# Copies of packed heads from gl into pkt: issued on GpSimd in place of VectorE

## The chip, the cores and the metric

The program runs on one core of a Trainium2 chip, in one launch. The metric is the device time of one execution in microseconds (us). The engines are named as in the profile: PE is TensorE's matmul stream and PEld its weight loads, DVE is VectorE, ACT is ScalarE, POOL is GpSimd, SP is SyncE, which here only issues DMAs. POOL issues DMAs too.

## The reference

Three layers follow each other. The first packs the sequence into 32 rows for each head and attends to them:

```python
def sm_attn(qq, kk, vv):                      # softmax attention, scale 1/8
    ...
p_packed = sm_attn(p, k, v)                   # (4, 8, 32, 64): 32 packed rows per head
out = sm_attn(q, p_packed, p_packed)          # q: (4, 8, 576, 64)
```

The second is a mixture of 4 experts on the 2304 tokens (512 wide, 1024 hidden): `out += p[:, e] * (relu(x @ w1[e]) @ w2[e])`. The third is a soft mixture: `logits = x @ phi` (32 slots), a softmax over the tokens gives 32 slot inputs, each goes through one of 8 experts of the same shape, and a softmax over the slots distributes the results. All is float32, and the result is (2304, 512).

## The kernel before

The work is cut into 4 batches `b` of 576 tokens, and the 8 heads of a batch into two groups `g` of 4. Order is written out by hand: each engine runs its instructions in the order in which the Python code issues them, and waits on semaphores where a tile comes from another engine.

`attention(b, g, ...)` is a generator, one `yield` for each step. For one group its steps are, in the code's order: transpose p and both halves of k (DVE L305, L288), scores of the packed rows into the PSUM tile `sa` (PE L297), softmax, transposed probabilities into `etm` (ACT L336), packed heads into the PSUM tile `pv` (PE L346) and from there into `gl` (ACT L357). Then come the 8 copies of L366: four heads by two halves of the head's width, each 32 partitions by 32 columns, from partitions 64*(h%2)+32*dh of `gl` to partitions 32*h of `pkt`, which becomes a block matrix with zeros between. After them both halves of q are transposed (DVE L288), multiplied with `pkt` into the PSUM tile `sb` (PE L297), turned into `nat` (DVE L378), normalized by a second softmax (L385 to L395, POOL for the differences and products), transposed into `a2` (L400) and split into a high and a low part (L409, L410). `gl` has two buffers, one for even and one for odd batches; `pkt` has one part for each group.

The attention of batches 0's two groups runs first, in the order of the string HEAD, mixed with the preparation of `wphi`. From then on there is a main loop of 128 slots, 32 for each batch. One slot does `mm1` (12 matmuls of L473 into two PSUM tiles `h`, ACT's L477 into `ht`), and at every fourth slot `make_g` (16 matmuls of L443 into two PSUM tiles `g`, split by ACT L454 and DVE L455) and `logits` (L500). `flip_h` transposes the `ht` of an earlier slot into `hn` (DVE L483) and scales it there (POOL L484). In the same slots one step of each attention generator of the next batch runs: group 0 starts at slot 0 of 32, group 1 at slot 9 (OFF1). So the 8 copies come twice in a batch, six times in the loop. The PSUM tiles for `h`, `g`, `sa`, `sb` and `pv` take turns in four banks, so that a matmul into a bank waits until its last reader is done. The order inside a slot is that of the string ORDER:

```python
    ORDER = "FGLMSAP"    # flip, make_g, logits, mm1, softmax step, attention step, pool_slots
```

The loads of q, k, v and p for later groups are issued on POOL (L136, L143), from the list `due` that is worked off at the start of the next slot; a k, q or v tile is one of four buffers, so an issue waits for the last reader of its buffer. w1 comes through SP (L169). When a batch is done, `pool_slots` (PE L611) multiplies its `hn` into the slot sums. After the loop, the rest of the weights streams in through SP (L715) into buffers that the loop has freed, and the last layers are computed (L989 to L1124).

Of the kernel before, what the change touches and what calls it, by code (L numbers as in the profile page):

```python
# [18 lines left out]
def tile_packed_attention_moe_softmoe(  # L19
# [15 lines left out]
    pe, act, dve, pool, sp = nc.tensor, nc.scalar, nc.vector, nc.gpsimd, nc.sync  # L35
# [242 lines left out]
    def attention(b, g, feeds, ptb, pkb, etb, tmp, gp):  # L278
# [83 lines left out]
        for h in range(4):  # L362
            for dh in range(2):
                src = 64 * (h % 2) + 32 * dh
                o = 32 * (2 * ((h + g) % 2) + h // 2)
                dve.tensor_copy(  # L366
                    pkb[32 * h : 32 * h + 32, dh, o : o + 32],
                    glb[src : src + 32, 2 * g + h // 2, :],
                )
# [46 lines left out]
    def start_attention(b, g):  # L416
        feeds = {}
        nb, ng = (b, 1) if g == 0 else (b + 1, 0)

        def later(src, nm, hf, bb, gg):  # L420
            return lambda: load_half(src, nm, bb, gg, hf)

        for hf in range(2):
            feeds[f"q{hf}"] = later(q, "q", hf, b, g)
            if nb < NB:
                feeds[f"k{hf}"] = later(k, "k", hf, nb, ng)
                feeds[f"v{hf}"] = later(v, "v", hf, nb, ng)
        if nb < NB:
            f = feeds["k0"]
            feeds["k0"] = lambda: (load_p(nb, ng), f())  # L430
        return attention(b, g, feeds, pt, pkt[:, g], [etm], att_tmp, pool)
# [305 lines left out]
    with tc.manual_schedule():  # L737
# [58 lines left out]
        def head_tmp(tag, name):  # L796
            if tag == "kt":
                return ht_pool.tile([128, S], F32, tag="ht", name=name)
            return spare[tag]

        gens = {
            "0": attention(0, 0, {}, pt, pkt[:, 0], [etm, et_x[0]], att_tmp, dve),
            "1": attention(
                0, 1, {}, pp1, pkt[:, 1], [et1, et_x[1]], head_tmp,
                pool if GP1 == "pool" else dve,
# [347 lines left out]
```

## Time and profile before

| | |
|---|---|
| device time, 3 runs | median 549.1 us (548.97 to 549.73) |
| the profiled execution | 549.31 us, span 547.2 us, granted TensorE clock 0.983 of full speed |
| PE busy | 498.7 us, 91% of the span |
| DVE busy | 322.2 us, 59% |
| ACT busy | 240.0 us, 44% |
| POOL busy | 236.3 us, 43% |

The span runs from the first to the last instruction; the device time has some 2 us around it. A busy share is an average over stages with different limits: the head (to about 50 us), the loop (to about 440 us) and the tail, in which weights stream in. The chain of waits follows the instruction that ended last back to what released it, step by step. An idle time in brackets in a timeline is that of the engine just before the instruction, with what ended it.

### The profile page before, as it was taken

Reading aid. Unit: us, or ns where it says so; the run is one execution under the profiler, and the core shown is the slowest. Engines: PE = TensorE matmul, PEld = TensorE weight load, DVE = VectorE, ACT = ScalarE, POOL = GpSimd, SP = SyncE. Lnnn points to the kernel's source line nnn. Section 1 sums busy time; section 2 is a strip of 40 time slices with the busy share of each in tenths; the row PEclk is TensorE's granted clock in tenths of the full one; section 3 lists DMA queues with packets and bytes.
Section 4 is the critical chain, followed back from the end, with each engine's and each line's share of the span. In section 5 each row is a group of like instructions: output and inputs, shape, how many; then the busy total and the mean of one; then the engine's idle time right before and its main releaser. Section 6 shows DMA issues by size and latency. Waiting matters only on the chain.

```text
span 547.2 us, 12839 instructions
## 1 busy us (share of the span) xinstructions
PE 498.7 (91%) x5356; PEld 347.5 (63%) x5356; DVE 322.2 (59%) x623; ACT 240.0 (44%) x548; POOL 236.3 (43%) x246
## 2 busy tenths in 40 slices
PE   7898999989999999899998989999999977998882
PEld 5776787867865767687556768775787853222132
DVE  6475457776767776768776676666645434451051
ACT  3766564655452447365334654551454411120041
POOL 8212445676642557675335555842555612000000
PEclk9998999999999999999999999999999997998998
DMA  8997155352430443443205432360388369999998
GB/s 283 365 375 271 49 166 176 98 166 79 153 122 1 146 143 103 150 148 120 79 10 177 158 100 79 132 234 22 126 277 292 128 238 398 409 389 383 371 253 239
DMA packets 70874, 104.06 MB, mean 190 GB/s; under 512 B 4433, under 2 KB 50257, under 8 KB 70817
## 3 DMA queue, kind: packets, MB, share of 16 engines
q1 hardware_dynamic: 66992, 93.20, 49.2%
q0 software_dynamic: 3232, 9.75, 6.0%
q8 instruction: 42, 0.69, 0.5%
q10 hardware_dynamic: 592, 0.29, 0.2%
q14 instruction: 16, 0.12, 0.1%
HBM read 98.52 MB, written 4.72 MB: 189 GB/s over the span
## 4 chain that ended last, share of the span: by engine, by line
PE 54%; DVE 15%; DMA 14%; ACT 8%; issue 4%; POOL 3%; SPq 0%; POOLq 0%; DVEq 0%; ACTq 0%
PE h L473 26%; DMA ck<-in_moe_w_dram 7%; PE sl L611 6%; PE g L443 5%; PE lg L500 4%; DMA hn<-in_moe_w_dram 3%; DVE pkt L366 3%; PE sb L297 3%; ACT etm L336 3%; DMA k<-in_k_dram 3%; PE sa L297 2%; PE w2t L251 2%; DVE hn L483 2%; POOL hn L484 2%; PE pw L237 1%
## 5 line engine op out<-in xcount | busy, mean ns | idle before, releaser
L473 PE MATMUL h<-a,g 128*128 128x288 f32 x1536 | 227.6, 302 | 6.9 <-DVE g L455 4.5
L473 PEld LDWEIGHTS h<-a,g 128*128 128x128 f32 x1536 | 208.7, 188 | 33.4 <-issue 22.3
L484 POOL TENSOR_TENSOR hn<-hn,dp_sb 128x576 f32<-128x576 f32 x128 | 152.0, 1193 | 130.0 <-DVE hn L483 126.3
L477 ACT ACTIVATE ht<-h 128x288 f32<-128x288 f32 x256 | 103.7, 412 | 155.2 <-PE h L473 154.9
L483 DVE STREAM_TRANSPOSE hn<-ht 128x576 f32<-128x576 f32 x128 | 96.3, 758 | 50.2 <-ACT ht L477 50.0
L455 DVE TENSOR_TENSOR g<-g,g 128x512 fp32r<-128x512 f32 x64 | 41.1, 683 | 24.8 <-ACT g L454 24.8
L611 PE MATMUL sl<-hn,dpt 32*32 32x512 f32 x1152 | 48.2, 597 | 2.4 <-DVE dpt L572 2.0
L454 ACT CAST g<-g 128x512 fp32r<-128x512 f32 x64 | 34.3, 588 | 21.1 <-PE g L443 21.0
L500 PE MATMUL lg<-ht,wphi 128*32 128x288 f32 x512 | 37.8, 412 | 0.0
L443 PE MATMUL g<-w,gl 64*32 64x512 f32 x512 | 35.7, 601 | 0.4 <-ACT ht L477 0.2
L611 PEld LDWEIGHTS sl<-hn,dpt 32*32 32x32 f32 x1152 | 21.0, 103 | 22.3 <-issue 13.3
L500 PEld LDWEIGHTS lg<-ht,wphi 128*32 128x32 f32 x512 | 13.5, 109 | 32.7 <-issue 25.5
L366 DVE COPY pkt<-gl 32x32 f32<-32x32 f32 x64 | 22.8, 356 | 7.3 <-ACT gl L357 6.5
L346 PE MATMUL pv<-etm,v 128*64 128x64 f32 x468 | 19.0, 225 | 6.5 <-ACT etm L336 3.4
L410 POOL TENSOR_TENSOR a<-a,a 64x576 fp32r<-64x576 f32 x14 | 20.0, 1427 | 9.6 <-ACT a L409 8.8
L336 ACT COPY etm<-et 32x288 f32<-32x288 f32 x52 | 22.2, 428 | 1.6 <-DVE et L330 0.4
L346 PEld LDWEIGHTS pv<-etm,v 128*64 128x64 f32 x468 | 16.2, 137 | 10.6 <-ACT etm L336 5.7
L1074 PE MATMUL so<-hn,tacc 128*32 128x384 f32 (+1 forms) x80 | 18.5, 590 | 2.7 <-DMA hn<-in_moe_w_dram 2.5
L629 DVE TENSOR_TENSOR tacc<-sl,tacc 128x512 f32<-128x512 f32 (+2 forms) x32 | 15.3, 545 | 9.4 <-PE sl L611 9.4
L297 PE MATMUL sa<-k,pt 128*128 128x288 f32 x56 | 16.9, 428 | 3.7 <-DVE k L288 3.6
L256 ACT COPY hn<-w2t 128x512 f32<-128x512 f32 x32 | 17.3, 588 | 6.6 <-PE w2t L251 6.5
L251 PE MATMUL w2t<-ident,hn 128*128 128x128 f32 x128 | 18.3, 287 | 1.8 <-ACT hn L256 1.3
(180 smaller groups left out, 492.4 us busy)
## 6 DMA issues: line engine op xcount, KB each, us to landing
w<-in_moe_w_dram SPq DMA_DIRECT2D x32, 1024.0 KB, 5.4
hn<-in_moe_w_dram SPq DMA_DIRECT2D x42, 512.0 KB, 9.7
ck<-in_moe_w_dram SPq DMA_DIRECT2D x42, 512.0 KB, 8.0
hn<-in_moe_w_dram SPq DMA_DIRECT2D x14, 384.0 KB, 8.5
q<-in_q_dram POOLq DMA_DIRECT2D x12, 288.0 KB, 3.2
out_dram<-ob SPq DMA_DIRECT2D x11, 288.0 KB, 4.4
k<-in_k_dram POOLq DMA_DIRECT2D x10, 288.0 KB, 3.2
v<-in_v_dram POOLq DMA_DIRECT2D x10, 288.0 KB, 3.6
```

What stands on the lines that cost most here:

```text
L297: pe.matmul(ps[:, :HS], lhs[:, j, :], t[:, :, j, :], start=(j == 0), stop=(j == 1))
L336: act.copy(etb[hf % len(etb)][r, h % 2, :, 32 * (h // 2) : 32 * (h // 2) + 32], et[r, HB * hf : HB * hf + HB, :],)
L346: pe.matmul(pv[64 * par : 64 * par + 64, :64], vn[:, x, :], etb[hf % len(etb)][:, par, x, :], start=(hf == 0 and x == 0), stop=(hf == 1 an ...
L366: dve.tensor_copy(pkb[32 * h : 32 * h + 32, dh, o : o + 32], glb[src : src + 32, 2 * g + h // 2, :],)
L443: pe.matmul(pss[g][32 * ((c + 2 * g) % 4) : 32 * ((c + 2 * g) % 4) + 32, :], gl[b % 2][r, c, :], t[r, c], start=True, stop=True, tile_posi ...
L455: dve.tensor_tensor(out=lo, in0=pss[g], in1=hi.bitcast(F32), op=ALU.subtract)
L473: pe.matmul(ps[:, :HS], gg[:, l, g, e % 2, fs], r[:, ts], start=(g == 0 and t == 0), stop=(g == 1 and t == 2),)
L477: act.activation(out=ht[:, ts], in_=ps[:, :HS], func=AF.Relu)
L483: dve.transpose(out=own, in_=unturned.pop((n, kf, e)).rearrange("p (x t) -> p x t", t=32))
L484: pool.tensor_tensor(out=own, in0=own, in1=dp_sb[:, n // NU, :, e].unsqueeze(2).to_broadcast([128, NBLK, 32]), op=ALU.mult,)
L500: pe.matmul(lg_t[b, pr][32 * c : 32 * c + 32, :HS], wphi[:, 2 * i + kf, 32 * e : 32 * e + 32], ht_t[n, kf, e][:, HS * hf : HS * hf + HS], ...
L611: pe.matmul(pss[f][c : c + 32, :], dpt[r, x, :], hn[r, p0 : p0 + NU, x, 2 * ep : 2 * ep + 2].rearrange("p n e k f -> p n (e k f)"), start= ...
```

## The change

One line: the 8 copies of each group are issued on POOL's queue.

```diff
         for h in range(4):
             for dh in range(2):
                 src = 64 * (h % 2) + 32 * dh
                 o = 32 * (2 * ((h + g) % 2) + h // 2)
-                dve.tensor_copy(
+                pool.tensor_copy(
                     pkb[32 * h : 32 * h + 32, dh, o : o + 32],
                     glb[src : src + 32, 2 * g + h // 2, :],
                 )
```

The 64 copies leave DVE's order and enter POOL's at the same place of the code. The orders of ACT and SP stay as they are; PE's too, but its `sb` matmuls now wait for POOL's semaphore where they took `pkt` from DVE.

DVE's order in the loop, where group 1 of batch 1 copies (`ht_0_1`, `ht_1_0` and `ht_1_1` are outputs of `mm1`, `q_1523` is the first transposed half of q):

```order
 L483 STREAM_TRANSPOSE hn<-ht_0_1_1427 128x18x32 [waits Activation_49]
 L483 STREAM_TRANSPOSE hn<-ht_1_0_1452 128x18x32 [waits Activation_49]
-L366 COPY pkt<-gl_114 32x32 [waits Activation_49]
-L366 COPY pkt<-gl_114 32x32 x7
 L288 STREAM_TRANSPOSE q_1523<-q_1157 128x576 [waits DMASW5_49]
 L483 STREAM_TRANSPOSE hn<-ht_1_1_1498 128x18x32 [waits Activation_49]
```

The transposes of q and of `ht_1_1`, and the two L455 behind them, now follow the transpose of `ht_1_0` directly.

POOL's order at the same place of the program (`k_1494` and `v_1525` are loads for batch 2, L484 scales `hn`):

```order
 L143 DMA k_1494<-in_k_dram 128x576 [waits DMASW0_49,PE_49]
 L484 TENSOR_TENSOR hn<-hn,dp_sb 128x18x32 [waits DVE_49,Pool_49]
+L366 COPY pkt<-gl_114 32x32 [waits Activation_49]
+L366 COPY pkt<-gl_114 32x32 [waits Pool_49]
+L366 COPY pkt<-gl_114 32x32 x6
 L143 DMA v_1525<-in_v_dram 128x576 [waits DMASW5_49,DVE_49]
-L484 TENSOR_TENSOR hn<-hn,dp_sb 128x18x32 [waits DVE_49]
+L484 TENSOR_TENSOR hn<-hn,dp_sb 128x18x32 [waits DVE_49,Pool_49]
```

The copies stand behind a load of k and a scaling, and in front of a load of v and the next scaling.

DVE's order where group 0 of batch 1 copies (`k_1153` and `k_1188` are the transposed halves of k for group 1, `q_1186` is the first of q for group 0):

```order
 L288 STREAM_TRANSPOSE k_1153<-k_1060 128x576 [waits DMASW3_49]
 L483 STREAM_TRANSPOSE hn<-ht_0_1_1113 128x18x32 [waits Activation_49]
-L366 COPY pkt<-gl_114 32x32 [waits Activation_49]
-L366 COPY pkt<-gl_114 32x32 x7
 L288 STREAM_TRANSPOSE q_1186<-q_803 128x576 [waits DMASW0_49]
 L288 STREAM_TRANSPOSE k_1188<-k_1155 128x576 [waits DMASW4_49,DVE_49]
```

The second half of k, which group 1's `sa` matmuls read, now stands two transposes behind the first.

## Rows read from the trace of the kernel before

**Rows 1.** The profile's page, part 4: the chain's shares of the span, by line.

```profile
PE h L473 26%; DMA ck<-in_moe_w_dram 7%; PE sl L611 6%; PE g L443 5%; PE lg L500 4%; DMA hn<-in_moe_w_dram 3%; DVE pkt L366 3%; PE sb L297 3%; ACT etm L336 3%; DMA k<-in_k_dram 3%; PE sa L297 2%; PE w2t L251 2%; DVE hn L483 2%; POOL hn L484 2%; PE pw L237 1%
```

**Rows 2.** The page, part 5: group xcount | busy us, mean ns | idle before, releaser.

```profile
L484 POOL TENSOR_TENSOR hn<-hn,dp_sb 128x576 f32<-128x576 f32 x128 | 152.0, 1193 | 130.0 <-DVE hn L483 126.3
```

**Rows 3.** Line L366: engine op xcount: ns min/median/max, first and last start us.

```profile
L366 DVE COPY pkt<-gl x64: 126/174/1637, 20.8 to 326.0; 32x32 f32<-32x32 f32 x64
```

**Rows 4.** Waits of PE, whole span: us in total, times, longest us.

```profile
PE h L473 <- DVE g L455: 4.5, 3, 1.5
```

**Rows 5.** Timeline of PE, 112 to 123 us: start, us, engine line op, tiles, xcount [idle before].

```profile
119.05 1.86 PE L473 MATMUL h<-a,g 128*128 128x288 f32 x12 [1.54 <-DVE g L455]
...
120.75 1.13 PE L297 MATMUL sb<-q,pkt 128*128 128x288 f32 x4
```

**Rows 6.** Timeline of DVE, 80 to 128 us.

```profile
112.91 4.05 DVE L366 COPY pkt<-gl 32x32 f32<-32x32 f32 x8 [0.86 <-ACT gl L357]
...
117.69 0.73 DVE L483 STREAM_TRANSPOSE hn<-ht 128x576 f32<-128x576 f32 x1
...
118.35 1.25 DVE L455 TENSOR_TENSOR g<-g,g 128x512 fp32r<-128x512 f32 x2
```

**Rows 7.** The chain that ended last, 110 to 123 us: start, us, what.

```profile
113.67 1.31 DVE pkt L366
...
115.65 1.11 DVE pkt L366
```

**Rows 8.** Timeline of POOL, 80 to 128 us.

```profile
112.02 2.93 POOL L410 TENSOR_TENSOR a<-a,a 64x576 fp32r<-64x576 f32 x2 [0.39 <-ACT a L409]
...
115.55 1.18 POOL L484 TENSOR_TENSOR hn<-hn,dp_sb 128x576 f32<-128x576 f32 x1
```

**Rows 9.** Timeline of ACT, 80 to 128 us.

```profile
113.64 0.41 ACT L477 ACTIVATE ht<-h 128x288 f32<-128x288 f32 x1 [0.39 <-PE h L473]
...
114.71 1.07 ACT L454 CAST g<-g 128x512 fp32r<-128x512 f32 x2 [0.66 <-PE g L443]
```

**Rows 10.** Timeline of DVE, 184 to 204 us.

```profile
188.22 2.84 DVE L366 COPY pkt<-gl 32x32 f32<-32x32 f32 x8
...
191.09 0.78 DVE L288 STREAM_TRANSPOSE q<-q 128x576 f32<-128x576 f32 x1
...
191.79 0.74 DVE L288 STREAM_TRANSPOSE k<-k 128x576 f32<-128x576 f32 x1
```

**Rows 11.** Timelines of PE, 184 to 204 and 288 to 306 us.

```profile
192.68 1.21 PE L297 MATMUL sa<-k,pt 128*128 128x288 f32 x4 [1.15 <-DVE k L288]
...
197.63 1.13 PE L297 MATMUL sb<-q,pkt 128*128 128x288 f32 x4
...
298.34 1.21 PE L297 MATMUL sa<-k,pt 128*128 128x288 f32 x4 [1.65 <-DVE k L288]
```

**Rows 12.** Timelines of POOL, 184 to 204 and 288 to 306 us.

```profile
187.93 0.58 POOL L143 DMA_DIRECT2D k<-in_k_dram  x1 [2.18 <-DVE k L288]
...
189.06 1.20 POOL L484 TENSOR_TENSOR hn<-hn,dp_sb 128x576 f32<-128x576 f32 x1
...
293.59 0.58 POOL L143 DMA_DIRECT2D k<-in_k_dram  x1 [2.67 <-DVE k L288]
```

**Rows 13.** DMA issues at 187.93 and 293.59 us: xcount, KB, us to landing.

```profile
k<-in_k_dram POOLq DMA_DIRECT2D x1, 288.0 KB, 3.1
...
k<-in_k_dram POOLq DMA_DIRECT2D x1, 288.0 KB, 3.2
```

**Rows 14.** Line L213 on POOL: xcount: ns min/median/max, first and last start us.

```profile
L213 POOL COPY hn<-ident x8: 198/202/202, 440.8 to 441.8; 128x16 f32<-128x16 f32 x8
```

**Rows 15.** Waits of SP's DMA queue: us in total, times, longest us.

```profile
SPq L715 <- PE sl L611: 8.7, 1, 8.7
```

**Rows 16.** Timelines of POOL, 0 to 24 us, and of DVE, 0 to 52 us.

```profile
14.00 3.58 POOL L181 DMA_DIRECT2D dp_sb<-in_moe_domain_probs_dram  x7 [0.57 <-DMA dp_sb<-in_moe_domain_probs_dram]
...
25.82 0.48 DVE L378 STREAM_TRANSPOSE nat<-sb 128x288 f32<-128x288 f32 x1 [2.09 <-PE sb L297]
```

## Prediction

> **What bounds the kernel now.** I read the chain of waits first. PE's h matmuls hold the largest part of it, and the 64 copies of L366 are on it with 3%, some 16 us, although they are a small group [rows 1]. So DVE's copies do hold something up, and the question is how much of that PE can get back. The line's own durations come next: a copy takes 174 ns at the median but up to 1637 ns [rows 3]. Two of the long ones stand in the chain: they end at 114.98 (113.67 plus 1.31) and at 116.76 (115.65 plus 1.11) [rows 7]. POOL's L410 pair ends at 114.95 and its L484 at 116.73 [rows 8]. A DVE copy that meets a POOL instruction ends with it: these copies don't compute, they wait for POOL. The transposes on DVE don't do that: L483 takes 0.73 us [rows 6].
>
> Then I look for what PE waits for. In the loop the copies come in two kinds of place, three times each, and both cost PE something. I call them stretch A (group 0; the rows show the second, at 188 us) and stretch B (group 1; the rows show the first, at 113 us).
>
> In stretch B eight copies hold DVE for 4.05 us from 112.91, so L455, behind them in DVE's order, starts only at 118.35 [rows 6], and PE stands still for 1.54 us until 119.05 [rows 5]. PE's waits for L455 before an h matmul are 4.5 us in 3 times over the whole span [rows 4]: these three places and no others.
>
> In stretch A the copies take 2.84 us, then come a transpose of q and the second half of k at 191.79 [rows 10]. PE's sa matmuls wait for that half: 1.15 us before 192.68, and 1.65 us before 298.34 one batch later [rows 11]. At the first of the three places I count no such wait.
>
> **The change part by part.** *DVE in stretch B.* Without the copies DVE is free at 112.05 (112.91 less its idle 0.86) [rows 6]. The q transpose (0.78, as in [rows 10]) runs to 112.8. The next L483 needs ACT's second ht half, ready at 114.05 [rows 9], and ends at 114.8. L455 then needs ACT's casts, of which both are done at 115.78 [rows 9], and its two parts of 1.25 us together [rows 6] end at 116.6 to 117.0. PE needs them at 119.05 less 1.54, that is 117.51 [rows 5]. The wait goes, with half a microsecond to spare or more. What is late next is nothing on DVE: PE goes straight on. Three places give 4.5 us.
>
> *DVE in stretch A.* Here something else is late next. The load of k's second half is issued on POOL at 187.93, after a wait for the transpose that frees its buffer, and it lands 3.1 us later [rows 12, 13], at 191.03. Without the copies, DVE reaches that transpose at about 189.0 (188.22 plus 0.78 for q [rows 10]), and stands until 191.03. The transpose ends 0.76 us sooner than before (191.79 less 191.03), and PE's sa sooner by the same if nothing else holds it, so 1.15 shrinks to 0.4: a gain of 0.76. One batch later the load is issued at 293.59 and lands after 3.2 us [rows 12, 13], at 296.79. From landing to sa it takes 0.89 us (192.68 less 191.79 [rows 10, 11]), so sa starts at 297.68 in place of 298.34 [rows 11]: 0.66. Together 1.4 us of the 2.8 us of waiting. The other half stays, under another name: the load of k.
>
> *POOL.* It gets 64 copies of 32 by 32. The trace has no copy of this form on POOL. The nearest is L213 (128 by 16, on the same engine): eight start within 1.0 us, 0.14 us apart, and the last takes 0.20 [rows 14], so a set of eight takes 1.2 us. The other end is POOL's two-input form over 576 columns, 1.193 us [rows 2], so 9.5 us a set. I take 1.2, because the work per partition is 32 elements, nearer to L213's 16 than to 576. It can't be below nothing: POOL does none of it now.
>
> A set on POOL costs nothing while it ends before the sb matmuls that read pkt. In stretch B POOL's L484 in front of the copies ends at 116.73 [rows 8], and sb, which stood at 120.75 [rows 5], moves up by the 1.54 to 119.2. That is 2.48 us for a set: 1.3 us to spare, and the cover is gone if one copy costs over 0.31 us. Then PE waits at sb, and with it every h matmul behind it. In stretch A POOL is free at 190.26 [rows 12], and sb comes at 196.9 (197.63 less 0.76) [rows 11]: 6.6 us for a set. Behind the copies in POOL's order wait a load of v and the next L484. In stretch A the load waits for the q transpose, done at 191.87 [rows 10], and now can go at about 191.5, so it isn't later. In stretch B it may be some 0.2 us later. hn and v are read only by matmuls of later stages, which is cover enough.
>
> *Head.* Two sets leave DVE. There the wait goes the other way: DVE stands 2.09 us for PE's sb matmuls [rows 16]. POOL's last head load is issued at 17.6 [rows 16], so it takes the copies at once. I count nothing.
>
> *The port.* Stretch B shows DVE's copies waiting for POOL's instructions; DVE's transposes and POOL's L484 run side by side at their usual times. So in their new place the copies have only transposes, which don't wait for POOL, and L455 beside them. The Trainium skill says (Perfetto Trace Analysis, Optimizing Scalar/DVE Operations) that GpSimd and VectorE share a port which some VectorE instructions hold exclusively, so that offloading from one to the other might not help. By that rule the set on POOL would be stalled as it was on DVE and the time would stay near 548 to 549; by the rows it wouldn't, and the sum is the one below. The trace agrees with the lock itself: copies of 1.31 and 1.11 us against a median of 0.174.
>
> *Sum.* 4.5 plus 1.4 is 5.9 us. The profiled execution took 549.3 us by its span of 547.2 and some 2 us around it; the median of the three runs is 549.1. So 543.4 against the one and 543.2 against the other; I forecast 543.2. The loop's gain has to pass through the tail, which streams weights. Its DMA issues wait for PE: one waits 8.7 us for the sl matmuls that close the loop [rows 15], so the stream starts sooner with PE.
>
> **The rivals.**
> *All waits go.* If k's load lands sooner once DVE's copies no longer run beside its issue, 2.8 us go in stretch A, 7.3 in all: 541.8. Against it: 3.1 and 3.2 us of landing are nothing slow, and the issue itself hangs on the earlier transpose.
> *The lock turns round.* POOL's copies wait for DVE as DVE's did for POOL, and a set takes the same 4.05 us. Then it overruns the 2.48 us in stretch B by 1.57, three times 4.7 us, of 5.9: 548.0. For it speaks that the waiting between the two engines is real; against it that POOL's L484 takes 1.18 us in this stretch and 1.193 on the mean of all 128 [rows 2, 8]. This is what the Trainium skill's rule on offloading, above, would do here.
> *The tail takes it back.* If the weight stream alone sets the end, the loop's gain turns into idle time at its end: 549.1. ck and hn loads hold some 10% of the chain [rows 1]; against it stands the SP wait above.
> *POOL's copy is dear: slower.* pkt then is late at sb. With p for one copy, stretch B loses three times (8p less 2.48), which eats the 5.9 us at p of 0.56 us. At L484's 1.193 a set takes 9.5 us: late by 7.1 in each stretch B and by 2.9 in each stretch A, 30 us less 5.9, so 573. For it: source and target partitions differ in most copies, and no POOL row shows such a copy. Against it: p would have to be four times L213's.
>
> **How the numbers follow.** Forecast 0.68, with its own range of 542.3 to 544.6; all waits go 0.10; lock 0.09; tail 0.06; dear copy 0.07. The range from 541.6 to 547.0 leaves out the last two and most of the lock, together some 0.20. A measurement of this kernel tells about 0.2%, 1.1 us, from no change. Faster by more: forecast, all waits, and half of the lock, 0.83. The same: the rest of the lock and the tail, 0.10. Slower: 0.07.
>
> **What the profile after would show.** L366 on POOL with eight starts within 1.2 us; no PE wait for L455 at the three places of stretch B; PE's sa still waiting some 0.4 and 1.0 us in the second and third stretch A, with DVE's k transpose now ended by the DMA; sb without a wait for POOL; the first tail load some 6 us sooner. A wait of sb on pkt would prove me wrong on POOL's price; an unchanged end of span with a shorter loop, on the tail.

## The result: 1.4% faster, more than the forecast range

| | before | changed |
|---|---|---|
| median of the runs | 549.4 us (548.97 to 550.19) | 541.7 us |
| the profiled execution | 549.31 us, span 547.2 | 541.67 us, span 539.6 |
| ratio to before, 95% interval | | 0.9853 (0.9836 to 0.9869) |

One execution of the changed kernel took 907.8 us; it is left out of the ratio. The forecast was 543.2 us, and its range ended at 541.6. The ratio puts the kernel at 541.0 against the 549.1 of the forecast, and a second comparison further down (0.9866) at 541.7: the sign and the mechanism came out, the gain was larger (about 8 us, or 7.4 by the second comparison, against 5.9).

The profile after, its page first: busy us, and the chain that ended last by engine and by line.

```profile
PE 497.0 (92%) x5356; PEld 346.1 (64%) x5356; DVE 300.1 (56%) x559; ACT 240.0 (44%) x548; POOL 248.5 (46%) x310
...
PE 65%; DVE 11%; DMA 8%; ACT 8%; issue 3%; POOL 3%; SPq 0%; POOLq 0%; DVEq 0%; ACTq 0%
PE h L473 30%; PE sl L611 7%; PE lg L500 5%; PE g L443 5%; DMA hn<-in_moe_w_dram 3%; ACT etm L336 3%; PE hid L1026 3%; PE pv L346 3%; PE sb L297 3%; PE sa L297 2%; DMA k<-in_k_dram 2%; DMA ck<-in_moe_w_dram 2%; PE si L989 1%; DVE hn L483 1%; PE w2t L251 1%
```

The copies are off the chain, where they had 3% [rows 1]; PE's h matmuls hold 30% of it where they held 26%. Line L366 now, on POOL (ns min/median/max):

```profile
L366 POOL COPY pkt<-gl x64: 200/204/218, 21.1 to 320.6; 32x32 f32<-32x32 f32 x64
```

No copy takes longer than 218 ns, where one on VectorE took up to 1637 [rows 3]. The long ones were waits, and GpSimd's copies have none. The trace of before bears this out for every long copy: all twelve over 0.5 us end 0.03 to 0.05 us after an L410 or L484 of POOL, while the 16 copies of the head, beside which POOL runs nothing, take 178 ns at most:

```profile
L366 DVE COPY pkt<-gl x16: 127/174/178, 20.8 to 27.5; 32x32 f32<-32x32 f32 x16
```

PE's waits for k's transposes (us in total, times, longest), before and then changed:

```profile
PE sa L297 <- DVE k L288: 4.7, 6, 1.6
```

```profile
PE sa L297 <- DVE k L288: 2.8, 6, 0.8
```

Of the 2.8 us only 0.82 stand in a stretch A. The wait of h for L455, 4.5 us in 3 times [rows 4], is gone from the list altogether. Stretch B on PE:

```profile
108.60 1.71 PE L346 MATMUL pv<-etm,v 128*64 128x64 f32 x36 [0.28 <-ACT etm L336]
...
114.17 3.45 PE L473 MATMUL h<-a,g 128*128 128x288 f32 x24
117.45 1.13 PE L297 MATMUL sb<-q,pkt 128*128 128x288 f32 x4
```

24 h matmuls run on where 1.54 us of idle time stood between two dozens [rows 5], and sb follows without a wait. The same stretch on DVE, and then on POOL:

```profile
109.77 0.78 DVE L483 STREAM_TRANSPOSE hn<-ht 128x576 f32<-128x576 f32 x1 [1.61 <-ACT ht L477]
110.47 0.74 DVE L288 STREAM_TRANSPOSE q<-q 128x576 f32<-128x576 f32 x1
112.59 0.78 DVE L483 STREAM_TRANSPOSE hn<-ht 128x576 f32<-128x576 f32 x1 [1.38 <-ACT ht L477]
113.84 1.29 DVE L455 TENSOR_TENSOR g<-g,g 128x512 fp32r<-128x512 f32 x2 [0.47 <-ACT g L454]
```

```profile
114.03 1.18 POOL L484 TENSOR_TENSOR hn<-hn,dp_sb 128x576 f32<-128x576 f32 x1
115.16 1.94 POOL L366 COPY pkt<-gl 32x32 f32<-32x32 f32 x8
117.05 0.58 POOL L143 DMA_DIRECT2D v<-in_v_dram  x1
```

DVE waits for ACT there and no longer PE for DVE. POOL's set takes 1.95 us and ends at 117.10, 0.35 us before sb: in time, with less to spare than the 1.3 us forecast. Stretch A, DVE and then PE:

```profile
184.95 0.73 DVE L288 STREAM_TRANSPOSE q<-q 128x576 f32<-128x576 f32 x1
187.74 0.78 DVE L288 STREAM_TRANSPOSE k<-k 128x576 f32<-128x576 f32 x1 [2.06 <-DMA k<-in_k_dram]
```

```profile
188.67 1.21 PE L297 MATMUL sa<-k,pt 128*128 128x288 f32 x4 [0.46 <-ACT ht L477]
...
291.70 1.21 PE L297 MATMUL sa<-k,pt 128*128 128x288 f32 x4 [0.82 <-DVE k L288]
```

DVE now stands 2.06 us until the load of k lands, as forecast, and PE's waits before sa are 0.46 and 0.82 us, where 1.15 and 1.65 stood [rows 11]. The row at 188.67 names ACT's ht, but sa starts there 0.15 us after the end of k's transpose (187.74 plus 0.78), as it did before (191.79 plus 0.74, and 192.68), so it is k here too.

### The profile page after: what moved, and what is told of

Same layout as the page of the kernel before. It is cut to its first block, busy times and chain, and to the rows that moved or that the text cites. A ratio compares the mean times of both kernels' runs of the same rounds, so it can differ in the third digit from the quotient of the medians.

```text
span 539.6 us, 12853 instructions
## 1 busy us (share of the span) xinstructions
PE 497.0 (92%) x5356; PEld 346.1 (64%) x5356; DVE 300.1 (56%) x559; ACT 240.0 (44%) x548; POOL 248.5 (46%) x310
## 4 chain that ended last, share of the span: by engine, by line
PE 65%; DVE 11%; DMA 8%; ACT 8%; issue 3%; POOL 3%; SPq 0%; POOLq 0%; DVEq 0%; ACTq 0%
PE h L473 30%; PE sl L611 7%; PE lg L500 5%; PE g L443 5%; DMA hn<-in_moe_w_dram 3%; ACT etm L336 3%; PE hid L1026 3%; PE pv L346 3%; PE sb L297 3%; PE sa L297 2%; DMA k<-in_k_dram 2%; DMA ck<-in_moe_w_dram 2%; PE si L989 1%; DVE hn L483 1%; PE w2t L251 1%
## 5 line engine op out<-in xcount | busy, mean ns | idle before, releaser
L484 POOL TENSOR_TENSOR hn<-hn,dp_sb 128x576 f32<-128x576 f32 x128 | 151.6, 1191 | 123.1 <-DVE hn L483 118.8
L455 DVE TENSOR_TENSOR g<-g,g 128x512 fp32r<-128x512 f32 x64 | 41.1, 684 | 26.6 <-ACT g L454 26.6
L410 POOL TENSOR_TENSOR a<-a,a 64x576 fp32r<-64x576 f32 x14 | 19.9, 1424 | 9.6 <-ACT a L409 8.9
L378 DVE STREAM_TRANSPOSE nat<-sb 128x288 f32<-128x288 f32 x14 | 6.8, 483 | 25.3 <-PE sb L297 25.3
L631 DVE SCALAR_TENSOR_TENSOR tacc<-tacc,rsc,sl 128x384 f32<-128x384 f32 (+2 forms) x20 | 9.2, 527 | 17.3 <-PE sl L611 17.3
```

Source lines behind the costliest of these rows:

```text
L455: dve.tensor_tensor(out=lo, in0=pss[g], in1=hi.bitcast(F32), op=ALU.subtract)
L484: pool.tensor_tensor(out=own, in0=own, in1=dp_sb[:, n // NU, :, e].unsqueeze(2).to_broadcast([128, NBLK, 32]), op=ALU.mult,)
```

## The experiments

To see where a gain arises, I divided PE's timeline in every run into the same pieces: from the start of the last pv matmuls ahead of a set of copies to the start of the second sb group behind it. In the profile of before the first stretch A so goes from 82.41 to 96.48 us, and the first stretch B from 110.11 to 123.30. The table has what each piece is shorter than in the profile of before, in us, summed over the three of its kind.

```
run                    stretches A   stretches B
before, once more          0.21          0.00
only the head              0.29          0.01
only stretches B           0.35          5.23
only stretches A           1.80          0.02
the changed kernel         1.91          5.24
the same, once more        2.36          5.21
a reduce on VectorE        1.89          5.24
copies twice on GpSimd     2.16          1.43
k's first half on SP       1.93          5.27
the same, once more        3.66          5.26
both halves on SP          3.66          5.28
```

Stretches B repeat within 0.02 us where the copies stay as they were, and within 0.07 us where their wait is gone. Stretches A scatter more: by up to 0.35 us with unchanged copies, and by 0.45 between two profiles of the changed kernel, where the landing of a load ends the wait.

**The kernel before, once more.** No edit.

> The kernel before, unchanged, profiled once more. In the profile of before TensorE's granted clock is at its lower level (0.50) from 51 to 54 us, in the first h and w2t matmuls of the loop, and in the profile of after it isn't; that is worth 1.5 us of the 7.6 us between the two spans. Theory 'chance': the dip comes and goes from one execution to the next whatever engine copies; then this profile may show it or not, and the times of before spread by about 1.5 us. Rival 'the change removes it': the dip at 51 us is here again, and in every profile with the head's copies on VectorE.

549.11 against 548.64 us, ratio 1.000 (0.998 to 1.002). The windows from 49 to 57 us (busy us of PE, PEld, DVE, ACT, POOL, then granted clock, DMA share, GB/s) of the first profile of before, of this run, and of the next kernel:

```profile
49.00:57.00 8.00, 6.85 (x38) 6.14 (x39) 6.33 (x20) 4.74 (x10) 3.31 (x4) 0.79 0.44 138
```

```profile
49.00:57.00 8.00, 6.21 (x64) 5.51 (x67) 6.43 (x20) 5.76 (x13) 3.32 (x4) 1.00 0.44 137
```

```profile
49.00:57.00 8.00, 6.75 (x37) 6.05 (x38) 6.36 (x20) 4.66 (x10) 3.33 (x4) 0.79 0.45 139
```

Mean granted clock 0.79, 1.00, 0.79: in the first and the third, PE runs at the lower of its two levels (0.50 of full speed) for some 3 us, right after it stood idle twice for POOL's L410, in h and w2t matmuls of the first slot. In the second it stood idle there just so and kept its clock. The same program shows the dip once and once not, and the last kernel below, with all copies on GpSimd, shows it too (0.79 in the same window), so it doesn't hang on the change: it is chance, and so are 1.5 us of the difference between the first two spans. A comparison of two single profiles would have put them down to the change; the medians don't depend on it.

**Only stretches B on GpSimd.**

```diff
-                dve.tensor_copy(
+                (pool if b and g else dve).tensor_copy(
```

> Only the copies of group 1 of batches 1 to 3 (the three stretches B) are issued on GpSimd; the other 40 stay on VectorE. Theory: a stall of PE costs more than the idle time in its row, since matmuls that follow without a stop overlap by some 0.2 to 0.3 us; PE gains 1.75 us at each of three places, 5.2 us in all: about 543.9 against 549.1. Rival 'the idle rows are the whole price': 4.5 us, 544.6. The milestones of PE tell them apart: from the pv matmuls before to the sa matmuls after each stretch B 1.75 or 1.50 us less than before.

542.96 against 548.64, ratio 0.9894 (0.9869 to 0.992). The interval holds both 5.2 and 4.5 us; the table decides: 5.23 us, 1.74 a place, the theory and not the 4.5 us of the idle rows. Before shows why (PE's timeline, start and length in us):

```profile
115.66 1.85 PE L473 MATMUL h<-a,g 128*128 128x288 f32 x12
119.05 1.86 PE L473 MATMUL h<-a,g 128*128 128x288 f32 x12 [1.54 <-DVE g L455]
```

From 115.66 to 119.05 are 3.39 us for 12 matmuls and the wait. In the changed kernel 24 take 3.28 us, from 114.17 to 117.45 above, so 12 take 1.64 and the wait is 1.75. The row says 1.54, because it counts from the end of the matmul before (115.66 plus 1.85), and a matmul that needn't wait starts before that end.

**Only stretches A on GpSimd.**

```diff
-                dve.tensor_copy(
+                (pool if b and not g else dve).tensor_copy(
```

> Only the copies of group 0 of batches 1 to 3 (the three stretches A) are issued on GpSimd. Theory: PE gains until the load of k's second half lands, 0.37, 0.70 and 0.84 us, 1.9 us in all: about 547.2 against 549.1. Rival 'the waits of the stretches A go wholly': 0.4 plus 1.15 plus 1.65 plus overlap, 3.3 us or more: 545.8.

546.50 against 548.64, ratio 0.9959 (0.9943 to 0.9975). By the table 1.80 us: 0.38, 0.65 and 0.77. The waits don't go wholly.

**Only the head on GpSimd.**

```diff
-                dve.tensor_copy(
+                (dve if b else pool).tensor_copy(
```

> Only the 16 copies of batch 0 (the head) are issued on GpSimd. Theory: nothing of the head waits for them, the time stays within 0.5 us of before, and the clock at 51 to 54 us is at either level by chance. Rival: the head's copies bring or remove the lower clock at 51 us; then the time is 1.5 us less, 547.6, and the profile shows full clock there in every execution.

548.34 against 548.64, ratio 0.9995 (0.9979 to 1.0011): nothing. Its profile has full clock at 51 us, but so has before once more.

**The changed kernel, once more.**

> The changed kernel once more, to size its gain against the same before as the three partial kernels. The parts measured so far: stretches B 0.9894, stretches A 0.9959, head 0.9995 of before. Theory 'the parts add up': product 0.985, about 540.5 against 548.6. Rival 'they overlap' (the same idle time is won twice): the gain is at most that of stretches B, 0.989 to 0.991.

541.76 against 549.26, ratio 0.9866 (0.9842 to 0.9889). The product of the three parts is 0.9849. They add up within the intervals.

**The copies on VectorE, as a reduce.**

```diff
-                dve.tensor_copy(
-                    pkb[32 * h : 32 * h + 32, dh, o : o + 32],
-                    glb[src : src + 32, 2 * g + h // 2, :],
-                )
+                dve.tensor_reduce(
+                    out=pkb[32 * h : 32 * h + 32, dh, o : o + 32],
+                    in_=glb[src : src + 32, 2 * g + h // 2, :].unsqueeze(2),
+                    axis=AX.X, op=ALU.max,
+                )
```

> The copies stay on VectorE, in the old order, but each is written as a tensor_reduce over a last axis of length 1. Theory: what cost PE was not that VectorE makes 64 copies but that a VectorE COPY waits for the GpSimd instruction beside it; a reduce doesn't wait, a set takes some 1.5 us in place of 2.84 and 4.05, L455 in stretch B is done half a microsecond before PE needs it and in stretch A the load of k decides: nearly the whole gain, 541 to 542.5. Rival 'VectorE's queue is simply too long there': the sets stay as long as before or PE waits for L455 and k as before, 547 to 549.

542.82 against 549.26, ratio 0.9883 (0.986 to 0.9907); its interval and that of the changed kernel overlap. Line L366 in this kernel, then the first stretch B on DVE:

```profile
L366 DVE TENSOR_REDUCE pkt<-gl x64: 130/177/182, 20.6 to 316.5; 32x32 f32<-32x32 f32 x64
```

```profile
110.87 1.51 DVE L366 TENSOR_REDUCE pkt<-gl 32x32 f32<-32x32 f32 x8 [0.85 <-ACT gl L357]
```

64 instructions on the same engine, at the same places, with the same data, and the longest takes 182 ns in place of 1637; a set takes 1.51 us in place of 4.05 [rows 6], while POOL runs its L410 pair (L411 in this file) beside it as before:

```profile
109.98 2.92 POOL L411 TENSOR_TENSOR a<-a,a 64x576 fp32r<-64x576 f32 x2 [0.41 <-ACT a L410]
```

The gain in both kinds of stretch is that of the changed kernel. So what cost PE was not VectorE's work on the copies but the form COPY, which waits for a running GpSimd instruction. The Trainium skill states it so (SBUF — State Buffer, Who interferes with whom): a copy can take the second pair of ports, which VectorE shares with GpSimd, and whichever of the two issues first keeps it for its whole instruction, while a tensor_reduce on trn2 never contends for it. The trace agrees on the two forms: 182 against 1637 ns at most. On who comes first it is less plain: in the second stretch A of before a copy starts at 188.72, while POOL still issues loads and ahead of its L484 at 189.06, and yet it ends with that L484 (190.30 and 190.26).

**Each copy twice on GpSimd.**

```diff
-                dve.tensor_copy(
-                    pkb[32 * h : 32 * h + 32, dh, o : o + 32],
-                    glb[src : src + 32, 2 * g + h // 2, :],
-                )
+                for _ in range(2 if b else 1):
+                    pool.tensor_copy(
+                        pkb[32 * h : 32 * h + 32, dh, o : o + 32],
+                        glb[src : src + 32, 2 * g + h // 2, :],
+                    )
```

> The copies on GpSimd, and in batches 1 to 3 each one is issued twice. Theory: a set takes 3.9 us in place of 1.95; in stretch B GpSimd is free 2.3 us before the sb matmuls, so they wait 1.6 us and some 0.25 us of lost overlap at three places, 5.5 us: about 546.5 against 541 for the changed kernel; stretch A has cover enough. Rival 'the copies have ample cover everywhere': within 0.5 us of the changed kernel.

545.57 against 549.26, ratio 0.9936 (0.9911 to 0.9961): 3.8 us over the changed kernel in the same set of runs. POOL in the first stretch B, PE there, and PE's waits:

```profile
115.38 4.05 POOL L367 COPY pkt<-gl 32x32 f32<-32x32 f32 x16
```

```profile
118.94 1.29 PE L297 MATMUL sb<-q,pkt 128*128 128x288 f32 x4 [1.14 <-POOL pkt L367]
```

```profile
PE sb L297 <- POOL pkt L367: 2.9, 3, 1.1
```

The place and the mechanism are those forecast, and the table has 3.8 us less gain in stretches B and none less in A. The size was off (5.5 expected): the waits are 1.14, 1.12 and 0.61 us, where 1.6 was expected at each place. One reason is that sb starts at 118.94, before the set ends at 119.43: its first matmul reads only the half of `pkt` with `dh` 0, which is complete with the 14th of the 16 copies, at 118.89, some 0.5 us before the last. The other is that POOL issues a load of k (0.58 us) shortly before the copies in the first two places and not in the third, which is about the difference between them.

**p and k's first half through SP, ahead of the w1 load,** on top of the changed kernel, and the same file once more.

```diff
-                due.append(feeds[key])
+                due.insert(0 if key == "k0" else len(due), feeds[key])
...
-            f = feeds["k0"]
-            feeds["k0"] = lambda: (load_p(nb, ng), f())
+            # p and the first half of k go through SP
+            feeds["k0"] = lambda: (load_p(nb, ng, sp), load_half(k, "k", nb, ng, 0, eng=sp))
```

> The changed kernel, and the loads of p and of k's first half go through SP's queue, ahead of the w1 load of the same slot. Theory: in stretch A the chain is first half landed (6 us beside the w1 load), transposed, buffer free, second half issued on GpSimd, landed, transposed, sa; with the first half landing 2 to 3 us sooner PE's waits of 0.46 and 0.82 us before sa go, 1.3 us and some overlap: 0.2 to 0.3% under the changed kernel, about 539.5 to 540. Rival 'another link decides': transposes of p or the issue on GpSimd hold the second half, and the time is that of the changed kernel.

> The kernel with p and k's first half on SP, once more. In its first profile PE's wait before sa went at the second stretch A, but at the third it was 1.5 us, since k's second half, issued on GpSimd, took 5.3 us to land where it takes 3.1 to 3.2 elsewhere. Theory 'a straggler by chance': here the third stretch A has a landing near 3.2 us and no wait over 0.5 us, and the time is 540.2 or less. Rival 'a standing collision of loads': 5 us and a wait of some 1.5 us again at the same place.

540.22 against 549.26, ratio 0.9848 (0.982 to 0.9876), and once more 539.93 against 549.70, ratio 0.9832 (0.9806 to 0.9857). At the second stretch A PE's wait before sa is gone in both profiles: k's second half is issued at 183.57 in the second of them, where the second profile of the changed kernel, with PE's last pv matmuls ahead of it at the same 181.95, has 184.51. In the first profile the wait of the third stretch A was longer, not shorter (1.49 us where 0.82 stood): k's second half, issued at 285.44, landed late. DMA issues at that place (KB, us to landing) in the first and the second profile:

```profile
k<-in_k_dram POOLq DMA_DIRECT2D x1, 288.0 KB, 5.3
```

```profile
k<-in_k_dram POOLq DMA_DIRECT2D x1, 288.0 KB, 3.1
```

The straggler did not come again, and with 3.1 us PE's sa starts without a wait there:

```profile
290.21 1.13 PE L297 MATMUL sa<-k,pt 128*128 128x288 f32 x4
```

What delayed the load in the one execution stays open.

**Both halves of k through SP,** on top of the kernel just shown (that kernel's line with a minus).

```diff
-                due.insert(0 if key == "k0" else len(due), feeds[key])
+                due.insert(0 if key in ("k0", "k1") else len(due), feeds[key])
...
+            feeds["k1"] = lambda: load_half(k, "k", nb, ng, 1, eng=sp)
```

> As k_first, and k's second half is issued through SP too. Theory: the second half is issued by the same release of its buffer, and lands 2 to 3 us later without GpSimd's share in it: PE's waits before sa go at all three stretches A, 0.2 to 0.3% under the changed kernel, about 539.5 to 540.2. Rival: SP's queue holds it behind a w1 load, then the waits before sa are those of the changed kernel or longer, 541.5 or more.

540.09 against 549.70, ratio 0.9827 (0.98 to 0.9855): the same as with the first half alone, in the table too. The waits had gone already, so nothing was left to win. Both versions are the fastest here. Beside the changed kernel (0.9853 and 0.9866) the intervals overlap, so the step from it is shown by the table, 3.66 against 1.91 and 2.36 us, rather than by the times.

## Why the prediction was right in sign and too small

- *PE stands for VectorE's copies in stretch B, and the wait goes wholly.* Right, and shown by the partial kernel. "Three places give 4.5 us" is the step that failed first, a term of the sum sized too small: they give 5.2, since the idle time in PE's row leaves out the overlap of matmuls that follow each other, 0.2 to 0.25 us a stop.
- *"At the first of the three places I count no such wait."* Wrong for the same reason, a term put at nothing: 0.36 us came from there, where PE's row shows no idle time.
- *Stretch A: the load of k decides, half of the waiting stays.* Right as a mechanism: DVE stands for the DMA, and PE waits 0.46 and 0.82 us where 0.4 and 1.0 were forecast. The three places give 1.9 to 2.4 us where 1.4 was said for two.
- *The sum.* 5.9 became 7.1 to 7.6 us by the table; the medians say 7.5 to 7.7. In the two single profiles 1.5 us more come from the clock, by chance, 0.4 us are lost in the head ahead of the first copy (the first pv matmuls start at 14.20 in place of 13.83), and 0.9 us are given back in the tail, where PE waits for weights: from the start of its first transposes (L961) to that of its output matmuls (L1112) 69.05 us before and 69.96 after. Against the first profile of before, that tail piece goes from 1.2 us shorter to 1.0 us longer over the runs, so it isn't a price of the change that could be told from chance.
- *A set on POOL takes 1.2 us.* It takes 1.95. The row was the nearest one, and its spacing of 0.14 us did not carry over: 0.25 here. The cover held it, with 0.35 us to spare.
- *The head costs nothing.* Right.
- *The rivals.* All waits go: its time, 541.8, is what was measured, but its mechanism did not come; only with k's first half on SP do these waits go. The lock turns round: no, the longest copy on POOL took 218 ns (its sum comes to 547.9, not 548.0). The tail: the stream of weights behind the loop starts 8.3 us sooner (438.22 against 446.53), so the loop's gain passes through; the tail takes back the 0.9 us above at most. The dear copy: no, though a doubled one shows the mechanism at work.

The step that failed is thus the price of a stop of PE, read from its idle time alone: 4.5 for 5.2 us in stretches B, nothing for 0.36 us at the first stretch A. The range was built on the same rows, and its low end is those rows added up, so all its cases were too small together. What is left between the 7.1 to 7.6 us of the table and the 8 us of the first ratio is within that ratio's interval (7.2 to 9.0 us).

## What to carry to other kernels

Where instructions of one line have a median of 0.17 and a maximum of 1.6 us, look at what the neighbour engine runs at the long ones: here another form on the same engine won as much as the move to another engine. Price a stop of PE by the starts of the groups before and after it, against the same group where it runs on, not by the idle time in its row. And before two single profiles are compared piece by piece, profile one of them again: here 1.5 us of the difference was a clock that fell in one execution of a program and not in the next.

## What was not expected of the hardware

- GpSimd copies of 32 by 32 and of 128 by 16 both report some 0.20 us, but eight of them start 0.25 and 0.14 us apart. The Trainium skill warns of this (Perfetto Trace Analysis, GPSIMD Engine Instruction): GpSimd's reported spans should be replaced by the spacing of starts. The trace agrees, with 0.20 against 0.14 and 0.25.
- One load of 288 KB on GpSimd's queue took 5.3 us where the same place took 3.1 in the next profile. The length as such is nothing rare: the loads of k that POOL issues in the first two stretches B (114.89 us and 218.60 in before) took 4.9 to 5.8 us in every profile that has them.
